# A dynamic convolution with LayerNorm and FFN: W1's last channels loaded as half rows in order, the first chunk summed by GpSimd and out of PSUM by VectorE, W1 split from PSUM, and a planner that lets transfers share engines

## The chip, the core and the metric

The kernel runs on one core of a Trainium2 chip. The metric is the device time of one execution in microseconds; the kernel before takes 903.2 us, the median of three runs (901.89 to 903.55).

## What is computed

```python
w = softmax(weight_gen, axis=-1)          # 8 x 4224 x 8 heads x 7 taps
x_pad = concat([zeros((B, 6, D)), x], 1)  # D = 192, 24 channels per head
y = einsum('bshk,bskhg->bshg', w, x_unf)  # each token: 7 taps over itself and the 6 tokens before
xn = (y - mean) / sqrt(var + 1e-6) * g_ln
out = y + relu(xn @ w_ch1) @ w_ch2        # 192 -> 768 -> 192
```

W1 and W2 come as 64-bit floats; the kernel reads them as pairs of 32-bit words and makes float32 of them. The products keep float32 accuracy with float16 operands: each operand is split into a high and a low half, and three products are summed.

## The kernel before

Each of the 128 partitions holds 264 consecutive tokens. They are worked in *parts* (six of 4 tokens, six of 8, fifteen of 12, then 8 and 4), each part in *chunks* of 4 or 6 tokens, and for the FFN in *groups* of 4 tokens, 66 in all.

A chunk (`conv`, L389) is seven products of x with the softmax weights in PSUM (tile wn), on VectorE: three pairs (taps 1 and 2, 3 and 4, 5 and 6) into tiles `pr`, of which there are five, and tap 0 into y. The sum: two accumulating DMAs issued by GpSimd (`pr<-pr`, L429) add one half of the first two pairs to the other, and four GpSimd additions (L426) bring everything into y. Then, per part, ScalarE takes sums and squares, and VectorE refines the reciprocal root in five small instructions (`newton`, L496 to L502); per group, ScalarE makes xh, its high half hl (L530), GpSimd the low half (L532), and a DMA transpose on SP's queue makes xT (three tiles). TensorE multiplies a group by W1 in three units of two PSUM banks (ph, two tiles); ScalarE and VectorE take each unit out (hh L576, hlo L578). W2's products go into po (L615 to L617), VectorE adds them to y (L628), and y goes out.

W1 (`load_weights`, L651; `weights`, L728) is three blocks of 128 rows in SBUF: channels 0 to 127, and twice a mix that pairs its rows with the last 64 channels, so that the wide products use all rows. The first load brings channels 0 to 127 (tile hh, 768 KB); the second (another hh, 384 KB) brings channels 128 to 191 as two sets of 64 rows, columns 0 to 383 on the upper partitions and 384 to 767 on the lower. `from_double` (L667) makes float32 of them, in PSUM first and then in tile hlo; ScalarE writes the high halves scaled by g and the scaled values themselves, GpSimd the low halves (L767), and twelve transfers on SP's queue (`shift`, L770) put the pieces into place. A first group can be transposed only behind them on that queue.

What sets the order: every operation is recorded with its engine, a cost and a due time, and `Plan.order` (L110) lays them out; engines, then, execute in the order that the plan gives. The due time is the token's number less a lead from the table WANT (two numbers per kind). The planner gives SP's and GpSimd's DMAs each a transfer line of its own, each 1.2 times as slow as alone, and keeps accumulating DMAs and transposes apart: neither starts while the other is under way, by waits in the program. SP's DMAs and ScalarE's use eight semaphores in turn, so each waits until the one eight before it has landed.

Of the kernel before, what the change touches and what calls it, by code (L numbers as in the profile page):

```python
# [16 lines left out]
P = 128  # L17
ALPHA = 8.0
NT = 4
# [3 lines left out]
EARLY = 0  # L23
CHUNK = 6
RING = 36
# [5 lines left out]
WANT = {'load': (-3.03, -19.38), 'wload': (75.89, -46.46), 'max': (34.08, -74.96), 'sub':  # L31
    (21.91, 116.2), 'exp': (-14.1, -87.13), 'sum': (39.61, 14.25), 'rcp': (47.36, -72.19),
    'inv': (5.5, -15.05), 'mul': (-41.29, 41.17), 'halo': (40.29, 5.8), 'c0': (31.82, 116.02),
    'c1': (-5.94, 64.81), 'c2': (-43.6, 83.75), 'c3': (-47.04, -21.22), 'd0': (9.3, 89.09),
    'd1': (-94.02, 26.89), 'a0': (-71.11, 94.32), 'a1': (-79.29, 54.26), 'a2': (-38.66, 25.11),
    'a3': (-85.55, -28.69), 'sums': (-195.22, -33.59), 'squares': (-140.38, 13.37), 'rstd':
    (10.58, 16.36), 'newton': (-103.15, -69.45), 'xh': (-25.48, -52.72), 'hi': (-57.47, -92.25),
    'lo': (-83.78, 4.64), 'turn': (28.46, -71.2), 'unit': (18.6, -32.95), 'relu': (-139.25,
# [3 lines left out]
    'w_load2': (-57.38, -12.17), 'w_as': (-60.92, -81.04), 'w_av': (-119.14, 5.54), 'w_an':  # L42
    (-33.01, 32.36), 'w_cs': (-238.15, 59.14), 'w_cv': (-62.73, -9.89), 'w_cn': (-11.28, 14.73),
    'w_c2s': (-60.02, 35.93), 'w_c2v': (-72.14, 39.45), 'w_c2n': (-110.82, -2.78), 'w_s1':
    (-187.12, 48.03), 'w_s2': (2.12, 17.57), 'w_h': (-21.92, -107.89), 'w_l': (-164.62, 27.59),
    'w_m': (-71.61, -95.38), 'w_h2': (13.94, -20.11), 'w_l2': (-164.98, -137.48)}
RAMP = 3.7
AHEAD = 0.0
WINDOW = 20.41
NEAR = 29.84  # L50
# [14 lines left out]
class Plan:  # L65
# [12 lines left out]
    def op(self, eng, cost, want, fn, r=(), w=(), lat=140.0, dma=0.0, kind=None):  # L78
# [5 lines left out]
        lead, more = WANT[want[0]]  # L84
        s = want[1]
        o.want = s - lead - more * max(0.0, 1 - s / RAMP)
# [21 lines left out]
    def order(self):  # L108
# [3 lines left out]
        last, clear = {"add": None, "turn": None}, {"add": 0.0, "turn": 0.0}  # L112
        for o in self.ops:
# [34 lines left out]
        while len(out) < len(self.ops):  # L148
# [22 lines left out]
            if o.dma:  # L171
# [3 lines left out]
                dma_free[o.eng] = begin + o.dma * (1.0 if o.kind == "turn" else 1.2)  # L175
# [16 lines left out]
def kernel(  # L192
# [61 lines left out]


# [9 lines left out]
    def dma_ns(n):  # L265
        return n * P / 250.0
# [7 lines left out]
    V.memset(bias[:, 0:1], 4e-6 / (ALPHA * ALPHA))  # L274
# [112 lines left out]

# [3 lines left out]
    def conv(c):  # L391
# [3 lines left out]
        prs = {k: Buf("pr") for k in (1, 3, 5)}  # L395
# [18 lines left out]
        def mul(k, nk):  # L414
# [4 lines left out]
            if k:  # L419
# [5 lines left out]
        def add(k, E=Q):  # L425
            E.tensor_tensor(out=flat(0), in0=flat(0), in1=flat(k), op=ALU.add)  # L426
# [4 lines left out]
        nd = n * D  # L431
# [3 lines left out]
        if c < EARLY:  # L435

            for i, (k, h) in enumerate(((1, 0), (1, 1), (3, 0), (3, 1), (5, 0), (5, 1))):
                op("Pool", q_ns(nd), (f"a{max(0, i - 2)}", t0), lambda k=k, h=h: add(k + h), [(prs[k], h)], yw)
            return
        for i, k in enumerate((1, 3)):  # L440
            op("Pool", 610, (f"d{i}", t0), lambda k=k: dma_add(k, k + 1), [(prs[k], 1)],
               [(prs[k], 0)], dma=600.0 + 400.0 * n, kind="add")
# [10 lines left out]
    def norm(pa):  # L453
# [29 lines left out]
        A2 = ALPHA / 2  # L483
# [6 lines left out]
        def root():  # L490
            A.activation(row(1), row(0), AF.Ln, scale=1.0 / (D * A2 * A2), bias=bias[:, 0:1])
            A.activation(row(1), row(1), AF.Exp, scale=-0.5)
            A.activation(row(2), row(1), AF.Square)

        def newton():
            V.tensor_scalar(out=aux(0), in0=row(0), scalar1=1.0 / (D * A2 * A2), scalar2=1e-6 / (A2 * A2),  # L496
                            op0=ALU.mult, op1=ALU.add)
            V.tensor_tensor(out=aux(1), in0=aux(0), in1=row(2), op=ALU.mult)
            for o in (aux(2), row(1)):
                V.scalar_tensor_tensor(out=o, in0=aux(1), scalar=3.0, in1=row(1), op0=ALU.subtract,  # L500
# [3 lines left out]
        op("ACT", 670, ("rstd", S0), root, vs, [(s4, "r")])  # L504
        op("V", 780, ("newton", S0), newton, [*vs, (s4, "r")], [(s4, "n"), "aux", *ms])
# [58 lines left out]
    W1S = ["h0", "l0", "h1b", "l1b", "l2t", "h2t"] + [(k, i) for k in ("h1t", "l1t", "h2b", "l2b") for i in range(2)]  # L564
# [75 lines left out]
    for name, shape, dt in (("g", [P, 2], F32), ("gi", [P, 2], F32), ("s1", [P, 4], F32),  # L640
                            ("s2", [P, 4], F32), ("r1", [P, 4], F32), ("r2", [P, 4], F32),
                            ("fs", [P, 1], F32), ("w1h", [P, 3, F], F16), ("w1l", [P, 3, F], F16),
                            ("w2h", [P, NF, D], F16), ("w2l", [P, NF, D], F16)):
        W[name] = cp.tile(shape, dt, name="c_" + name)
    for name in ("g", "s1"):
# [226 lines left out]
```

## Time and profile before

| | us |
|---|---|
| timed, three runs | 901.89, 903.2, 903.55 |
| profiled execution | 901.05 |
| its span | 899.2 |
| TensorE, VectorE, ScalarE, GpSimd busy | 813.2, 781.7, 675.7, 694.4 |
| first product of the first group | 53.02 |

The span runs from the first to the last instruction of the program. A busy TensorE isn't TensorE at its peak, since matmuls overlap: the count of matmuls in a stretch says more. An idle time stands with the instruction that follows it, and with what ended the wait.

### The profile page before, as it was taken

What the parts mean: (1) busy time and instruction counts of PE and PEld (TensorE: products, weight loads), DVE (VectorE), ACT (ScalarE), POOL (GpSimd) and SP (SyncE); (2) the same over time, 40 slices, a digit from 0 to 9 for tenths busy, and PEclk for the clock granted to TensorE, in tenths of its full rate; (3) what the DMA queues carried; (4) which work ended last, traced back from release to release, by engine and by line L of the source; (5) the groups of instructions that cost most, each with busy time, mean ns of one, the idle gap of its engine ahead of it and who ended that gap; (6) DMA issues with size and microseconds to landing.
All of it is one profiled execution on the core that took longest, in us unless ns stands there. A gap on an engine that the chain in (4) does not pass through costs nothing.

```text
span 899.2 us, 21468 instructions
## 1 busy us (share of the span) xinstructions
PE 813.2 (90%) x8716; PEld 728.8 (81%) x8716; DVE 781.7 (87%) x833; ACT 675.7 (75%) x1773; POOL 694.4 (77%) x403
## 2 busy tenths in 40 slices
PE   0037979999999999989999999999999999999997
PEld 0025969889898888888899988898899898889987
DVE  5799989999999999889999998999999799785332
ACT  1579877888878787788878778788788778788321
POOL 4499989998998896886987979689698598886000
PEclk9997999999999999999999999999999999999999
DMA  8875778878786878777788688787877867654212
GB/s 212 211 166 126 173 160 180 195 163 189 164 195 111 203 147 193 184 158 166 164 187 185 139 182 175 169 197 158 170 167 148 170 134 162 153 111 98 63 53 54
DMA packets 138604, 142.42 MB, mean 158 GB/s; under 512 B 107657, under 2 KB 109449, under 8 KB 138505
## 3 DMA queue, kind: packets, MB, share of 16 engines
q1 hardware_dynamic: 123513, 89.14, 42.0%
q0 software_dynamic: 14688, 51.91, 29.6%
q8 instruction: 68, 1.11, 0.5%
q14 instruction: 31, 0.25, 0.1%
q10 hardware_dynamic: 304, 0.00, 0.0%
HBM read 36.43 MB, written 25.95 MB: 69 GB/s over the span
## 4 chain that ended last, share of the span: by engine, by line
PE 26%; DVE 12%; POOL 9%; ACT 8%; DMA 6%; issue 5%; SPq 0%; POOLq 0%; DVEq 0%
PE ph L546 13%; POOL y L426 7%; DVE pr L423 7%; PE po L615 5%; PE po L617 4%; PE po L616 4%; DMA xT<-hl 3%; DVE hlo L578 3%; ACT hh L576 3%; ACT junk L468 2%; DMA pr<-pr 2%; ACT junk L463 1%; DVE y L423 1%; POOL hl L532 1%; DVE y L628 1%
## 5 line engine op out<-in xcount | busy, mean ns | idle before, releaser
L426 POOL TENSOR_TENSOR y<-y,pr 128x1152 f32<-128x1152 f32 (+1 forms) x204 | 503.6, 2475 | 82.0 <-DVE pr L423 70.5
L616 PE MATMUL po<-c_w2l,hh 128*128 128x192 f16 x1584 | 389.7, 246 | 1.4 <-POOL c_w2l L808 1.4
L615 PE MATMUL po<-c_w2h,hh 128*128 128x192 f16 x1584 | 390.1, 246 | 0.0
L617 PE MATMUL po<-c_w2h,hlo 128*128 128x192 f16 x1584 | 389.7, 246 | 0.0
L546 PE MATMUL ph<-xT,c_w1h 128*128 128x256 f16 x2376 | 328.3, 275 | 34.2 <-DMA xT<-hl 18.8
L423 DVE TENSOR_TENSOR pr<-x,wn 128x2304 f32<-128x2304 f32 (+1 forms) x153 | 337.4, 2215 | 8.3 <-DMA x<-in_x_dram 3.3
L546 PEld LDWEIGHTS <-c_w1h 128*128 128x128 f16 x2376 | 226.4, 98 | 76.4 <-issue 43.2
L578 DVE SCALAR_TENSOR_TENSOR hlo<-ph,hh 128x1024 f16<-128x1024 f32 x198 | 239.3, 1217 | 49.9 <-ACT hh L576 48.7
L576 ACT ACTIVATE hh<-ph 128x1024 f16<-128x1024 f32 x198 | 199.6, 1008 | 68.8 <-PE ph L546 46.0
L546 PE MATMUL ph<-xT,c_w1l 128*128 128x256 f16 (+1 forms) x1584 | 211.0, 274 | 9.8 <-DMA xT<-hl 8.9
L615 PEld LDWEIGHTS <-hh 128*128 128x128 f16 x1584 | 155.0, 98 | 7.8 <-issue 6.1
L616 PEld LDWEIGHTS <-hh 128*128 128x128 f16 x1584 | 155.1, 98 | 1.6
L617 PEld LDWEIGHTS <-hlo 128*128 128x128 f16 x1584 | 155.0, 98 | 1.6 <-issue 1.6
L514 ACT ACTIVATE xh<-y,s 128x192 f32<-128x192 f32 x264 | 123.3, 536 | 31.9 <-DVE s L502 28.3
L546 PEld LDWEIGHTS <-c_w1l 128*128 128x128 f16 (+1 forms) x1584 | 108.5, 96 | 41.8 <-issue 26.2
L532 POOL TENSOR_TENSOR hl<-xh,hl 128x768 f16<-128x768 f32 x66 | 118.8, 1868 | 15.9 <-ACT hl L530 15.8
L463 ACT ACTIVATE junk<-y 128x192 f32<-128x192 f32 x264 | 95.1, 360 | 42.4 <-POOL y L426 36.8
L468 ACT ACTIVATE junk<-y,s 128x192 f32<-128x192 f32 x264 | 119.5, 453 | 7.1
L429 POOL DMA_DIRECT2D pr<-pr x102 | 96.2, 1003 | 34.5 <-DVE pr L423 20.9
L628 DVE SCALAR_TENSOR_TENSOR y<-po,c_fs,y 128x384 f32<-128x384 f32 x132 | 79.8, 608 | 28.2 <-PE po L617 28.1
L530 ACT ACTIVATE hl<-xh 128x768 f16<-128x768 f32 x66 | 55.1, 835 | 8.2 <-DMA xT<-hl 7.6
L423 DVE TENSOR_TENSOR y<-x,wn 128x1152 f32<-128x1152 f32 (+1 forms) x51 | 60.0, 1178 | 0.0
(64 smaller groups left out, 327.2 us busy)
## 6 DMA issues: line engine op xcount, KB each, us to landing
pr<-pr POOLq DMA_DIRECT2D x60, 576.0 KB, 7.6
x<-in_x_dram SPq DMA_DIRECT2D x30, 576.0 KB, 7.0
out_dram<-y SPq DMA_DIRECT2D x30, 576.0 KB, 4.8
pr<-pr POOLq DMA_DIRECT2D x42, 384.0 KB, 6.6
out_dram<-y SPq DMA_DIRECT2D x21, 384.0 KB, 4.3
x<-in_x_dram SPq DMA_DIRECT2D x20, 384.0 KB, 6.6
w<-in_weight_gen_dram SPq DMA_DIRECT2D x21, 336.0 KB, 4.3
pr<-in_moe_w_ch_dram SPq DMA_DIRECT2D x1, 1152.0 KB
```

The costliest lines, as they stand in the source:

```text
L423: V.tensor_tensor(out=ov, in0=xv, in1=wv, op=ALU.mult)
L426: E.tensor_tensor(out=flat(0), in0=flat(0), in1=flat(k), op=ALU.add)
L463: A.activation(junk, at(y)[:, j, :], AF.Identity, scale=-1.0 / D, accum_out=at(s4)[:, 3, t : t + 1])
L468: A.activation(junk, at(y)[:, j, :], AF.Square, bias=at(s4)[:, 3, t : t + 1], accum_out=at(s4)[:, 0, t : t + 1])
L514: A.activation(at(xh)[:, t, :], at(y)[:, i, :], AF.Identity, bias=at(s4)[:, 3, g + t : g + t + 1], scale=at(s4)[:, 1, g + t : g + t + 1])
L532: lambda xh=xh, hl=hl: Q.tensor_tensor(out=halves(hl, True), in0=pairs(xh), in1=halves(hl, False), op=ALU.subtract),
L546: T_.matmul(at(gp["ph"][u])[:, r, v * 2 * P : (v + 1) * 2 * P], W[w][rows, wb, (2 * u + v) * P : (2 * u + v + 1) * P], xv[rows, r, xb, :, ...
L576: lambda: A.activation(at(hh)[:, us, :], at(ph), AF.Relu), [ph], [(hh, u)])
L578: lambda: V.scalar_tensor_tensor(out=at(hlo)[:, us, :], in0=at(ph), scalar=0.0, in1=at(hh)[:, us, :], op0=ALU.max, op1=ALU.subtract),
L615: T_.matmul(o, tok(hh, j), w2h[:, j, :], start=(j == 0), stop=False)
L616: T_.matmul(o, tok(hh, j), w2l[:, j, :], start=False, stop=False)
L617: T_.matmul(o, tok(hlo, j), w2h[:, j, :], start=False, stop=(j == NF - 1))
```

## The change

The second W1 load takes the half rows in the order of the tensor, so that a row's two halves lie on two neighbouring partitions; g's matching column is loaded in one transfer with each value twice. The float32 values of W1 stay in PSUM (ph for channels 0 to 127, po for the rest). The high halves are written from there as before; the low halves are now one VectorE instruction each (scale and subtract), the scaled copies are gone, and W1's high and low halves lie side by side in one tile, so that six transfers shift both at once, the last four picking every second partition.

Chunk 0 (`EARLY = 1`) has no accumulating DMAs: VectorE writes taps 5 and 6 into PSUM one by one and adds each to y, and GpSimd adds the other two pairs up among themselves and then to y. Newton's scaling is put into constants, which leaves four instructions, and the square goes to PSUM. The planner lets SP's and GpSimd's transfers that are under way together lengthen each other, knows of the eight semaphores, and the table WANT gives a lead at five token numbers; all its numbers are new.

```diff
-EARLY = 0
+EARLY = 1
...
-WANT = {'load': (-3.03, -19.38), 'wload': (75.89, -46.46), 'max': (34.08, -74.96), 'sub':
+KNOTS = (0, 4, 8, 16, 40)
+WANT = {'load': (169.34, 28.1, -223.88, -75.09, -80.57), 'wload': (125.01, 154.38, 150.29,
...
+            if o.dma:
+                before = lanes[o.eng == "Pool"]
+                if len(before) >= LANES:
+                    t = max(t, before[-LANES].end)
...
-                dma_free[o.eng] = begin + o.dma * (1.0 if o.kind == "turn" else 1.2)
+                dma_free[o.eng] = begin + o.dma
+                for e, x in latest.items():
+                    if e != o.eng and o.kind != "turn":
+                        both = min(max(0.0, dma_free[e] - begin), o.dma)
+                        dma_free[o.eng] += both
+                        dma_free[e] += both
...
+        if c < EARLY:
+            for i, k in enumerate((1, 3, 0)):
+                op("V", v_ns(2 * nd if k else nd), (f"c{i}", t0), lambda k=k: mul(k, 2 if k else 1),
+                   [*xr, "wn"], [(prs[k], 0), (prs[k], 1)] if k else yw)
+            for k in (5, 6):
+                ph = Buf("ph")
+                op("V", v_ns(nd), ("c3", t0), lambda k=k, ph=ph: mul(k, 1, ph), [*xr, "wn"], [ph])
+                op("V", v_ns(nd), ("c3", t0), lambda ph=ph: V.tensor_tensor(out=flat(0), in0=bank(ph)[:, :nd], in1=flat(0), op=ALU.add),
+                   [ph], yw)
+            for i, (a, b) in enumerate((((1, 0), (1, 1)), ((3, 0), (3, 1)), ((1, 0), (3, 0)), (None, (1, 0)))):
+                op("Pool", q_ns(nd), (f"a{i}", t0),
...
         def newton():
-            V.tensor_scalar(out=aux(0), in0=row(0), scalar1=1.0 / (D * A2 * A2), scalar2=1e-6 / (A2 * A2),
-                            op0=ALU.mult, op1=ALU.add)
-            V.tensor_tensor(out=aux(1), in0=aux(0), in1=row(2), op=ALU.mult)
+            V.scalar_tensor_tensor(out=aux(1), in0=row(0), scalar=D * 1e-6, in1=aux(0), op0=ALU.add, op1=ALU.mult)
...
         dma("SP", SY, "load", lambda: words(1, 0, F),
-            bass.AP(tensor=w1b.tensor, offset=P * 2 * F, ap=[[F, 2], [2 * F, 64], [1, F]]), 4 * F, raw[1])
+            bass.AP(tensor=w1b.tensor, offset=P * 2 * F, ap=[[F, P], [1, F]]), 4 * F, raw[1])
...
-        def low(dst, src, hi, n, r, w):
-            op("Pool", q_ns(n), ("w_l", 0), lambda: Q.tensor_tensor(out=dst(), in0=src(), in1=hi(), op=ALU.subtract), r, w)
+        def low(dst, src, scale, hi, n, r, w):
+            op("V", v_ns(n), ("w_l", 0), lambda: V.scalar_tensor_tensor(
+                out=dst(), in0=src(), scalar=scale, in1=hi(), op0=ALU.mult, op1=ALU.subtract), r, w)
...
-        halves(w1h, hc, [(raw[1], "h")], "h")
-        copy("w_h", lambda: f32(wa, F), lambda: f32(wa, F), F, ["gi"], [wa], gi[:, 0:1])
...
+        shift(w1[bot, 1], lambda: w1[top, 0], ["h0", "l0"], ["1b"])
+        shift(w1[top, 2], lambda: w1[bot, 0], ["h0", "l0"], ["2t"])
...
+            for dst, name in ((w1[top, 1, :, fs], "1t"), (w1[bot, 2, :, fs], "2b")):
+                shift(dst, lambda i=i: hlc()[i::2], [(raw[1], "h"), (raw[1], "l")], [(name, i)], F)
```

How the order moves, at three places. A number behind a name is the buffer; rows without a time stand in the order of their engine.

SP's queue at the start of the program, before (w: weights of the softmax, hh_88 and hh_89: W1's two loads):

```order
L341 DMA w_64<-in_weight_gen_dram 128x1x224
L323 DMA x<-in_x_dram 120x1x1920
L328 DMA x<-in_x_dram 8x768
L341 DMA w_65<-in_weight_gen_dram 128x1x448
L341 DMA w_66<-in_weight_gen_dram 128x1x672
L657 DMA hh_88<-in_moe_w_ch_dram 128x1536
L657 DMA hh_89<-in_moe_w_ch_dram 128x1x768
L341 DMA w_64<-in_weight_gen_dram 128x1x672
```

and in the changed kernel:

```order
L385 DMA w_64<-in_weight_gen_dram 128x1x224
L367 DMA x<-in_x_dram 120x1x1920
L372 DMA x<-in_x_dram 8x768
L710 DMA hh_88<-in_moe_w_ch_dram 128x1536
L710 DMA hh_89<-in_moe_w_ch_dram 128x768
L385 DMA w_65<-in_weight_gen_dram 128x1x448
L385 DMA w_66<-in_weight_gen_dram 128x1x672
L385 DMA w_64<-in_weight_gen_dram 128x1x672
```

W1's two loads stand ahead of the second and third w instead of behind them.

VectorE from chunk 0's first product on, before (L423: products; L361, L368: softmax; L689 to L699: W1 from double to float):

```order
L423 TENSOR_TENSOR pr_76<-x,wn_102 128x2x768
L423 TENSOR_TENSOR pr_77<-x,wn_102 128x2x768
L361 TENSOR_REDUCE mx_93<-w_65 128x64
L423 TENSOR_TENSOR y_67<-x,wn_102 128x768
L423 TENSOR_TENSOR pr_79<-x,wn_102 128x2x768
L368 TENSOR_REDUCE wn_102<-e_97 128x64
L689 TENSOR_SCALAR ph_103<-hh_88 128x768
L361 TENSOR_REDUCE mx_92<-w_66 128x96
L692 SCALAR_TENSOR_TENSOR ph_103<-hh_88,ph_103 128x768
L689 TENSOR_SCALAR ph_104<-hh_89 128x384
L695 SCALAR_TENSOR_TENSOR ph_103<-hh_88,ph_103 128x768
L692 SCALAR_TENSOR_TENSOR ph_104<-hh_89,ph_104 128x384
```

and in the changed kernel (L469: products, L485: sums out of PSUM, L744 to L754: W1):

```order
L469 TENSOR_TENSOR y_67<-x,wn_102 128x768
L469 TENSOR_TENSOR ph_103<-x,wn_102 128x768
L469 TENSOR_TENSOR ph_104<-x,wn_102 128x768
L485 TENSOR_TENSOR y_67<-ph_103,y_67 128x768
L485 TENSOR_TENSOR y_67<-ph_104,y_67 128x768
L744 TENSOR_SCALAR ph_103<-hh_88 128x768
L469 TENSOR_TENSOR pr_77<-x,wn_102 128x2x768
L747 SCALAR_TENSOR_TENSOR ph_103<-hh_88,ph_103 128x768
L750 SCALAR_TENSOR_TENSOR ph_103<-hh_88,ph_103 128x768
L754 SCALAR_TENSOR_TENSOR ph_103<-pr_78,ph_103 128x768
L405 TENSOR_REDUCE mx_93<-w_65 128x64
L744 TENSOR_SCALAR po_105<-hh_89 128x384
```

Chunk 0 begins with y and the two taps in PSUM, its product pairs (pr_77, and pr_79 in the next row) come later, behind pieces of W1's first load, and the second W1 load (hh_89) follows.

GpSimd around the low half of group 32, the third `hl` row, before (L426: sums into y, L429: accumulating DMAs, L363: softmax, L532: low halves):

```order
L532 TENSOR_TENSOR hl_83<-xh_81,hl_83 128x2x384
L532 TENSOR_TENSOR hl_84<-xh_82,hl_84 128x2x384
L426 TENSOR_TENSOR y_69<-y_69,pr_80 128x1152
L363 TENSOR_TENSOR e_96<-w_66,mx_92 128x672
L426 TENSOR_TENSOR y_69<-y_69,pr_80 128x1152
L532 TENSOR_TENSOR hl_83<-xh_81,hl_83 128x2x384
L426 TENSOR_TENSOR y_69<-y_69,pr_76 128x1152
L426 TENSOR_TENSOR y_69<-y_69,pr_78 128x1152
L429 DMA pr_77<-pr_77 128x1152
L429 DMA pr_79<-pr_79 128x1152
```

and in the changed kernel (L472, L475, L407, L584):

```order
L584 TENSOR_TENSOR hl_83<-xh_81,hl_83 128x2x384
L584 TENSOR_TENSOR hl_84<-xh_82,hl_84 128x2x384
L472 TENSOR_TENSOR y_72<-y_72,pr_78 128x1152
L407 TENSOR_TENSOR e_96<-w_66,mx_92 128x672
L584 TENSOR_TENSOR hl_83<-xh_81,hl_83 128x2x384
L475 DMA pr_77<-pr_77 128x1152
L472 TENSOR_TENSOR y_72<-y_72,pr_78 128x1152
L472 TENSOR_TENSOR y_72<-y_72,pr_76 128x1152
L475 DMA pr_80<-pr_80 128x1152
L475 DMA pr_79<-pr_79 128x1152
```

The transpose of group 32 waits for its low half and for the accumulating DMAs that the plan puts ahead of it. Before, there is none behind the low half that it waits for; now it is planned behind the three that follow (pr_77, pr_80, pr_79). The same comes again at groups 38, 44, 50 and 56.

More of the change, by code (lines that the diff above doesn't have):

```diff
@@ L18 @@
 ALPHA = 8.0
+ROOT_OF = (0.5 / (192 * ALPHA * ALPHA)) ** (1.0 / 3.0)
 NT = 4
@@ L53, with ahead_of @@
+AHEAD = 0.0
+WINDOW = 18.11
+NEAR = 19.46
+LANES = 8
+def ahead_of(key, s):
+    v = WANT[key]
+    for i in range(len(v) - 1):
+        if s < KNOTS[i + 1]:
+            return v[i] + (v[i + 1] - v[i]) * ((s - KNOTS[i]) / (KNOTS[i + 1] - KNOTS[i]))
+    return v[-1]
 class Buf:
@@ L174, in order @@
                             dma_free.get(o.eng, 0.0))
-                dma_free[o.eng] = begin + o.dma * (1.0 if o.kind == "turn" else 1.2)
+                dma_free[o.eng] = begin + o.dma
[4 more added lines that the diff above has]
+                        dma_free[e] += both
+                        x.end += both
+                        for d in x.nxt:
+                            d.ready = max(d.ready, x.end)
+                        if x.kind in clear:
+                            k = "turn" if x.kind == "add" else "add"
+                            clear[k] = max(clear[k], x.end)
+                latest[o.eng] = o
+                lanes[o.eng == "Pool"].append(o)
                 o.end = dma_free[o.eng] + self.DMA_END
@@ L562, in narrow_products @@
                        stop=(first and v == 1))
-    W1S = ["h0", "l0", "h1b", "l1b", "l2t", "h2t"] + [(k, i) for k in ("h1t", "l1t", "h2b", "l2b") for i in range(2)]
+    W1S = ["h0", "l0", "1b", "2t"] + [(k, i) for k in ("1t", "2b") for i in range(2)]
     def at_unit(unit):
@@ L786, in weights @@
-        shift(w1l[top, 2, :], lambda: w1l[bot, 0, :], ["l0"], ["l2t"])
-        copy("w_h", lambda: f32(wc, F2), lambda: f32(wc, F2), F2, ["gi"], [wc], gi[:, 1:2])
-        low(lc, lambda: f32(wc, F2), hc, F2, [wc, (raw[1], "h")], [(raw[1], "l")])
-        halves(w1l, lc, [(raw[1], "l")], "l")
+        def low(dst, src, scale, hi, n, r, w):
+            op("V", v_ns(n), ("w_l", 0), lambda: V.scalar_tensor_tensor(
+                out=dst(), in0=src(), scalar=scale, in1=hi(), op0=ALU.mult, op1=ALU.subtract), r, w)
@@ L791, in weights @@
+        shift(w1[top, 2], lambda: w1[bot, 0], ["h0", "l0"], ["2t"])
+        low(lambda: hlc()[:, 1], lambda: f32(wc, F2), gi[:, 1:2], lambda: hlc()[:, 0], F2, [wc, "gi", (raw[1], "h")],
+            [(raw[1], "l")])
+        for i in range(2):
+            fs = slice(i * F2, (i + 1) * F2)
+            for dst, name in ((w1[top, 1, :, fs], "1t"), (w1[bot, 2, :, fs], "2b")):
+                shift(dst, lambda i=i: hlc()[i::2], [(raw[1], "h"), (raw[1], "l")], [(name, i)], F)
         tn = NF // 3 * D
```

133 lines of the change are left out of this document (63 added, 70 removed), and 14 rows, old and new, of the table WANT.

## The prediction

> **What bounds the kernel now.** I read the page's first part, then the busy time by stretch, then the timeline of the start. The header of the stretches names each engine, its busy time and in brackets its instructions.
>
> ```profile
> span 899.2 us, 21468 instructions
> PE 813.2 (90%) x8716; PEld 728.8 (81%) x8716; DVE 781.7 (87%) x833; ACT 675.7 (75%) x1773; POOL 694.4 (77%) x403
> ...
> core 0: us, PE busy (x) PEld busy (x) DVE busy (x) ACT busy (x) POOL busy (x), PEclk, DMA share, GB/s
> ...
> 20.00:40.00 20.00, 0.59 (x2) 0.50 (x2) 12.81 (x23) 7.69 (x27) 8.21 (x7) 1.00 0.76 208
> 40.00:60.00 20.00, 6.52 (x45) 4.67 (x46) 19.35 (x32) 15.94 (x43) 17.50 (x12) 1.00 0.83 191
> 60.00:80.00 20.00, 9.51 (x56) 6.43 (x55) 19.69 (x28) 17.58 (x51) 19.24 (x13) 0.67 0.65 132
> 80.00:100.00 20.00, 18.62 (x202) 16.30 (x200) 18.73 (x27) 17.26 (x44) 20.00 (x14) 0.99 0.66 147
> 120.00:160.00 40.00, 35.29 (x380) 31.61 (x379) 37.06 (x45) 29.80 (x83) 35.92 (x25) 1.00 0.80 167
> 200.00:300.00 100.00, 98.58 (x1069) 88.80 (x1067) 97.38 (x102) 83.97 (x223) 89.96 (x53) 1.00 0.78 172
> 820.00:840.00 20.00, 20.00 (x220) 17.85 (x218) 8.68 (x14) 13.97 (x34) 4.74 (x3) 1.00 0.36 91
> ```
>
> With nothing to wait for (820 to 840 us) TensorE does 220 matmuls in 20 us, 11 per us. All 8716 at that rate are 792 us, so 107 us of the span are TensorE time lost, most of it before 80 us: 103 matmuls are done by then. From 80 us on TensorE is near its rate, but so is VectorE: busy 19.35, 19.69 and 18.73 of 20 us between 40 and 100, and 97.38 of 100 between 200 and 300. Up to 300 us the groups of tokens reach TensorE as fast as VectorE makes them. The start is where idle time is left:
>
> ```profile
> GB/s 0 77 133 288 199 225 263 313 272 243 250 229 236 268 180 37 53 50 108 298 384 305 253 250 253 255 254 224 209 240 98 155 72 67 261 172 283 250 225 205
> ...
> 26.75 0.56 DVE L689 TENSOR_SCALAR ph<-hh 128x384 int32<-128x384 int32 x1 [7.12 <-DMA hh<-in_moe_w_ch_dram]
> ...
> 49.67 1.55 SPq L536 DMA_TRANSPOSE xT<-hl  x1
> 53.02 1.44 PE L546 MATMUL ph<-xT,c_w1h 128*128 128x256 f16 x6 [18.76 <-DMA xT<-hl]
> ...
> 70.01 0.61 PE L546 MATMUL ph<-xT,c_w1l 64*128 64x256 f16 x4 [6.03 <-DMA xT<-hl]
> ...
> 81.57 0.24 PE L616 MATMUL po<-c_w2l,hh 128*128 128x192 f16 x1 [1.38 <-POOL c_w2l L808]
> ...
> 128.17 0.39 PE L546 MATMUL ph<-xT,c_w1l 64*128 64x256 f16 x4 [1.56 <-DMA xT<-hl]
> ```
>
> VectorE stands still for 7.12 us until W1's last 64 channels (tile hh, 384 KB) are there at 26.7 us. The first row is bytes per second in slices of 1.5 us from 0 to 60: around 13 to 21 us some 230 to 270 GB/s, then 37, 53 and 50 between 22.5 and 27. So the last load is not behind a full queue; it trickles by itself through a few transfer engines. TensorE begins at 53.02 with the first transposed group, and waits for groups again at 70.01 and 128.17.
>
> **The change, part by part.** Its durations, from the groups by shape, and the first and last of the twelve transfers that shift W1:
>
> ```profile
> L423 DVE TENSOR_TENSOR pr<-x,wn 128x1536 f32<-128x1536 f32 x63 | 108.9, 1745 | 6.7 <-DMA x<-in_x_dram 3.3 <-ACT rr L372 2.5 <-issue 0.5
> L423 DVE TENSOR_TENSOR y<-x,wn 128x768 f32<-128x768 f32 x21 | 19.7, 942 | 0.0
> L628 DVE SCALAR_TENSOR_TENSOR y<-po,c_fs,y 128x384 f32<-128x384 f32 x132 | 79.8, 608 | 28.2 <-PE po L617 28.1
> L699 DVE SCALAR_TENSOR_TENSOR hlo<-pr,ph 128x768 f32<-128x768 f32 x1 | 0.9, 946 | 0.0
> L699 DVE SCALAR_TENSOR_TENSOR hlo<-pr,ph 128x384 f32<-128x384 f32 x1 | 0.5, 544 | 0.0
> L496 DVE TENSOR_SCALAR wn<-s 128x12 f32<-128x12 f32 x15 | 2.4, 161 | 0.2
> L767 POOL TENSOR_TENSOR c_w1l<-hlo,c_w1h 128x768 f16<-128x768 f32 x1 | 1.6, 1630 | 0.0
> L767 POOL TENSOR_TENSOR hh<-hlo,hh 128x384 f16<-128x384 f32 x1 | 0.9, 905 | 0.0
> L429 POOL DMA_DIRECT2D pr<-pr x102 | 96.2, 1003 | 34.5 <-DVE pr L423 20.9 <-DMA xT<-hl 6.1 <-ACT c_r L716 3.1
> ...
> 41.41 1.17 SPq L770 DMA_DIRECT2D c_w1h<-c_w1h  x2
> 48.97 0.59 SPq L770 DMA_DIRECT2D c_w1l<-hh  x1
> ...
> 41.80 1.43 ACT L764 ACTIVATE hlo<-hlo,c_gi 128x768 f32<-128x768 f32 x2
> ```
>
> *The load.* W1's last channels are read as 128 half rows in their order instead of two sets of 64, and both W1 loads are issued ahead of the second and third w. The slices up to 12 us hold 2.25 MB, and the first w, x and W1 are 2.2 MB by their shapes; with 2 us to land I expect W1 on chip by about 14 us, when VectorE still has chunk 0 to do; the 7.12 us go. If the reordered load still lands late, nothing of this term is won; that end is kept. The Trainium skill, "DMA: Bandwidth & Descriptors", section "Why a DMA increments its semaphore by 16 and not by 1", says that a copy is split over the largest number of engines, up to 16, that divides the slowest dimension of both patterns. By it the old pattern (slowest dimension 2) runs on 2 engines and the new one on 16. The 37 to 53 GB/s agree with the first half; no run here shows the second.
>
> *Chunk 0 on VectorE.* One product pair (1.745) becomes two single products (2 x 0.942) into PSUM, and two sums out of PSUM come on top. A sum of that shape out of PSUM isn't in the trace: 0.942 as the same size in SBUF, 1.22 as twice the 608 ns of L628, half the size with one PSUM input. I take 0.942, the row of the right size: +1.88 - 1.75 + 1.88 = +2.0, at most +2.6. What GpSimd loses is two accumulating DMA issues (2 x 1.003).
>
> *W1's low halves* go from GpSimd (1.630 + 0.905) to VectorE: like L699, 0.946 + 0.544 = +1.5; the 608 ns of L628 against the 544 of L699, both 384 elements, price the PSUM source at below 0.1 more each. Two ScalarE copies (1.43 in sum, the last row above) go too; ScalarE is busy 15.94 of 20 us there, so I count them at nothing, and they would be worth at most their 1.43.
>
> *The shifts* become 6 transfers. The twelve hold SP's queue from 41.41 to 49.56, and the first transpose, queued behind them, is issued at 49.67. Six at about 0.6 us are 3.6: if the low halves are ready at about the same 42 us, the transpose waits for its own data, not for SP, and TensorE starts at some 50 instead of 53. That isn't added: the groups after it set the end.
>
> *Newton* loses one of five instructions, 0.16 us, in each of 29 parts. Twelve or thirteen parts lie before 300 us: -2.0. Behind that VectorE has idle time (8 us of the 92 after 354 us) and the saving is hidden.
>
> *Sum on VectorE up to 300 us:* -7.1 + 2.0 + 1.5 - 2.0 = **-5.6**. Bounds: -7.1 - 2.0 below if the PSUM work were free, +1.5 above if the load still comes late.
>
> *GpSimd.* It loses 2.0 + 2.5 us of work, but its first sums now wait for the product pairs, and VectorE does the single products and the sums out of PSUM ahead of those: five instructions of 0.942, 4.7 us. VectorE's products need the five pr buffers that GpSimd frees, so it will wait there once or twice after 65 us. That wait doesn't exist in the trace of before; between nothing and one sum (2.28 us, below) each, I take +1.0.
>
> *The steady part.* The order changes everywhere. What could be won is what TensorE loses there:
>
> ```profile
> 300.00:354.00 54.00, 51.47 (x555) 45.93 (x554) 50.98 (x51) 42.06 (x115) 43.19 (x23) 1.00 0.81 172
> 354.00:446.00 92.00, 88.76 (x962) 79.92 (x961) 83.78 (x79) 74.92 (x194) 77.69 (x42) 1.00 0.75 168
> ...
> 331.65 1.65 POOL L532 TENSOR_TENSOR hl<-xh,hl 128x768 f16<-128x768 f32 x1
> ...
> 341.06 1.34 POOL L429 DMA_DIRECT2D pr<-pr  x1
> ...
> 350.17 2.03 SPq L536 DMA_TRANSPOSE xT<-hl  x1
> ...
> 445.63 1.86 POOL L532 TENSOR_TENSOR hl<-xh,hl 128x768 f16<-128x768 f32 x1
> ...
> 468.87 0.82 PE L546 MATMUL ph<-xT,c_w1h 128*128 128x256 f16 x6
> ```
>
> At 11 per us these 555 and 962 matmuls are 50.5 and 87.5 us, so 3.5 and 4.5 are lost, 8.0 in all. One cause is seen for group 23: its low half ends at 333.3, but three accumulating DMAs are planned ahead of its transpose, the third is issued at 341.06, and the transpose leaves at 350.17. In the new order groups 23 and 26 are free of this, 25 and 20 wait for an add one row behind, and groups 32, 38, 44, 50 and 56 get the long form. I take -1.5 of the 8.0.
>
> **Forecast:** -5.6 + 1.0 - 1.5 = -6.1 us. The profiled execution took 901.05 us with its 1.85 us around the span; that gives 895.0. The median of the timed runs, 903.2, stands 2.15 above it, and I forecast that median: **897.1 us**. Chance 0.50, its own range 893 to 900.5.
>
> **Rivals.** *GpSimd becomes the bound.* For: it is busy 19.24 and 20.00 of 20 us between 60 and 100 us. Against: only 35.92 of 40 between 120 and 160, and 89.96 of 100 later, so it can catch up. Its own sum is -4.5 us of work and about half of the 4.7 us of later start, which it can't fill with other work, +2.5 as an estimate, -2.0 in all: 899.0, as a median 901.2. Chance 0.18. How its sums stretch:
>
> ```profile
> L426 POOL TENSOR_TENSOR y<-y,pr 128x768 f32<-128x768 f32 x4 | 7.2, 1805 | 2.2 <-DMA pr<-pr 1.2 <-DVE pr L423 1.0
> L426 POOL TENSOR_TENSOR y<-y,pr 128x768 f32<-128x768 f32 x14 | 31.7, 2282 | 0.7 <-DMA pr<-pr 0.5
> ```
>
> The first row is 16 to 27 us, where VectorE stood idle for 7, the second 60 to 100 us, where it was full. With VectorE filled, the four sums of chunk 0 could take 2.28 each, 1.9 us more. The Trainium skill, "GPSIMD Engine Reference", section "1. Specifications", has GpSimd's SBUF interface shared with VectorE and contended for by VectorE instructions with two SBUF inputs. By that rule the 1.9 us come, the sums out of PSUM excepted; it speaks for this rival, and the two rows agree with it, though DMA issues between the sums may stretch them too.
>
> *The steady losses go as well:* all 8.0 instead of 1.5 give -12.6, 888.4, as a median 890.6. For: the groups that lost most are re-ordered. Against: new long waits come in. Chance 0.13.
>
> *Slower: the five transposes behind adds decide.* Before, group 32's low half ended at 447.5 and TensorE began with it at 468.87, 21.4 us later. With group 23's detour (16.9 us from its low half to its transpose, and 3.4 until TensorE has it, as after 49.67) it would be there after 20.3. The margin is 1.1 us: the third add came 7.8 us behind the low half there, and from about 9 us on each further us is TensorE's. At 3 us late in each of five groups that is +15 - 6.1 = +8.9: 910.0, as a median 912. For: GpSimd's DMA issues wait for VectorE's products in the trace (20.9 us in all at L429). Against: group 23 itself was just in time. Chance 0.14.
>
> *The load is not faster:* W1's last channels again land at about 25 us, because of the traffic of the other loads. VectorE then only gains Newton's 2.0 and pays 3.5: +1.5, and with the rest 902 to 904. Against it are the 37 to 53 GB/s. Chance 0.05.
>
> **Chances.** Faster by over 0.2% (under 901.4; 0.2% is about what a measurement of this kernel can tell from no change): the forecast, the steady gain, and six tenths of the GpSimd case, 0.74. Within it: the rest of that case and the load's, 0.12. Slower: 0.14. The range reaches from the steady gain, 889, to 904; most of the slower case is left out.
>
> **What would show it.** VectorE's wait for hh (7.1 us) gone and W1's last load landed before 16 us; sums out of PSUM (128x768) of 0.94 to 1.22 us; TensorE's first group at about 50 us; VectorE over 95% busy from 15 to 300 us, with a few us waiting for GpSimd's pr. Wrong would be: a new wait of VectorE for GpSimd above 4 us before 100 us; TensorE waits for transposed groups around 470, 540, 615, 690 and 765 us; or a PSUM product that takes much longer than in SBUF.

## The result, and the profile after

The changed kernel takes **910.8 us** (median of four runs, 909.87 to 911.86), the kernel before 902.7 in the same session (901.89 to 903.55): a ratio of 1.009, with a 95% interval of 1.0072 to 1.0107. The forecast was 897.1 with a range up to 904. It is slower by 0.9%, and the forecast had the wrong sign.

The profile of the changed kernel begins:

```profile
span 908.9 us, 21412 instructions
...
PE 819.0 (90%) x8716; PEld 731.3 (80%) x8716; DVE 785.8 (86%) x809; ACT 671.9 (74%) x1771; POOL 692.0 (76%) x399
```

The start comes as early as forecast. In the changed kernel's timelines, ScalarE's and then VectorE's and TensorE's, W1's last channels are there at 12.5 us:

```profile
12.52 1.33 ACT L741 ACTIVATE pr<-hh 128x384 f32<-128x384 f32 x2 [6.80 <-DMA hh<-in_moe_w_ch_dram]
```

```profile
10.32 1.82 DVE L469 TENSOR_TENSOR ph<-x,wn 128x768 f32<-128x768 f32 x2
12.04 1.94 DVE L485 TENSOR_TENSOR y<-ph,y 128x768 f32<-128x768 f32 x2
13.91 0.95 DVE L744 TENSOR_SCALAR ph<-hh 128x768 int32<-128x768 int32 x1
...
19.88 0.55 DVE L744 TENSOR_SCALAR po<-hh 128x384 int32<-128x384 int32 x1
```

```profile
48.49 6.58 PE L598 MATMUL ph<-xT,c_w 128*128 128x256 f16 x40 [17.09 <-DMA xT<-hl]
...
62.97 1.36 PE L598 MATMUL ph<-xT,c_w 64*128 64x256 f16 x7 [5.07 <-DMA xT<-hl]
```

VectorE's L744 rows have no bracket: it waits for neither load. TensorE starts at 48.49 instead of 53.02. Busy time by stretch, in the changed kernel:

```profile
20.00:40.00 20.00, 0.59 (x2) 0.61 (x3) 19.04 (x30) 9.61 (x34) 17.17 (x12) 1.00 0.72 175
...
60.00:80.00 20.00, 12.42 (x83) 8.87 (x84) 18.80 (x17) 11.88 (x35) 16.66 (x11) 0.66 0.64 138
...
200.00:300.00 100.00, 93.98 (x997) 83.60 (x995) 93.34 (x96) 79.08 (x211) 87.19 (x51) 0.98 0.80 168
...
354.00:446.00 92.00, 91.58 (x987) 82.38 (x985) 85.80 (x84) 75.93 (x196) 78.26 (x42) 1.00 0.72 165
```

VectorE is busy 19.04 of 20 us between 20 and 40 (before 12.81). But where all engines were full before, between 200 and 300 us, VectorE, GpSimd and TensorE have all become idler: TensorE does 997 matmuls instead of 1069, and VectorE, at 93.34 of 100 us, is below the 95% that the prediction gave as a sign. Coarser stretches, first of the kernel before and then of the changed one, show where time is won and lost:

```profile
0.00:160.00 160.00, 90.52 (x897) 77.86 (x898) 138.67 (x191) 109.65 (x300) 128.16 (x92) 0.96 0.78 176
160.00:300.00 140.00, 137.12 (x1488) 123.41 (x1486) 136.52 (x144) 118.18 (x320) 129.01 (x79) 1.00 0.78 172
300.00:450.00 150.00, 144.22 (x1552) 129.09 (x1550) 137.90 (x133) 120.50 (x317) 124.88 (x66) 1.00 0.78 171
450.00:700.00 250.00, 248.96 (x2702) 224.74 (x2701) 236.89 (x228) 201.92 (x531) 209.16 (x111) 1.00 0.80 169
```

```profile
0.00:160.00 160.00, 95.79 (x936) 81.46 (x937) 146.11 (x190) 109.83 (x304) 125.21 (x88) 0.96 0.69 159
160.00:300.00 140.00, 132.26 (x1405) 117.58 (x1403) 131.50 (x135) 111.31 (x301) 124.41 (x77) 0.99 0.81 170
300.00:450.00 150.00, 147.37 (x1589) 132.45 (x1588) 139.60 (x130) 124.29 (x330) 127.44 (x68) 1.00 0.78 170
450.00:700.00 250.00, 241.21 (x2599) 217.02 (x2597) 226.37 (x211) 191.79 (x507) 200.84 (x106) 1.00 0.77 170
```

Against before, TensorE has done 39 matmuls more by 160 us, then 83 fewer, 37 more, and 103 fewer. At 11 per us the last is 9.4 us, and all four together are 10.0. So the loss lies in the steady part, where the prediction looked for a gain. The waits there (what waited, for whom: us in total, times, longest), first of before:

```profile
PE ph L546 <- DVE hlo L578: 16.2, 17, 3.1
...
ACT rr L372 <- DVE pr L423: 3.4, 2, 2.7
ACT rr L372 <- DVE y L423: 2.1, 3, 1.5
```

and of the changed kernel:

```profile
PE ph L598 <- DVE hlo L630: 26.9, 29, 4.6
...
ACT wn L547 <- DVE pr L469: 19.0, 15, 2.2
ACT rr L416 <- DVE pr L469: 18.4, 11, 3.7
```

TensorE waits longer for VectorE's low halves `hlo`, which free its PSUM tile ph. From 450 to 700 us alone, first before and then changed:

```profile
PE ph L546 <- DVE hlo L578: 0.2, 1, 0.2
```

```profile
PE ph L598 <- DVE hlo L630: 8.8, 11, 2.2
```

The 8.6 us more are most of the 9.4 us lost there. And ScalarE waits for VectorE's products `pr` at two places: at the square into wn (L547), a wait that before does not have, and at the softmax's Ln (L416, out rr), 18.4 us instead of 3.4. One wait of the latter kind, from VectorE's, ScalarE's and TensorE's timelines:

```profile
641.48 0.86 DVE L412 TENSOR_REDUCE wn<-e 128x96 f32<-128x672 f32 x1 [0.53 <-ACT e L410]
642.43 2.56 DVE L469 TENSOR_TENSOR pr<-x,wn 128x2304 f32<-128x2304 f32 x1
646.62 1.23 DVE L630 SCALAR_TENSOR_TENSOR hlo<-ph,hh 128x1024 f16<-128x1024 f32 x1 [1.63 <-ACT hh L628]
```

```profile
645.02 0.34 ACT L416 ACTIVATE rr<-wn,bias 128x96 f32<-128x96 f32 x1 [3.58 <-DVE pr L469]
645.39 0.28 ACT L417 ACTIVATE rr<-rr 128x96 f32<-128x96 f32 x1
645.58 1.00 ACT L628 ACTIVATE hh<-ph 128x1024 f16<-128x1024 f32 x1
```

```profile
647.90 1.36 PE L598 MATMUL ph<-xT,c_w 128*128 128x256 f16 x11 [1.63 <-DVE hlo L630]
```

The sums (L412) are done at 642.34. The Ln needs nothing else, but starts at 645.02, when the *next* product has ended (642.43 + 2.56 = 644.99). Behind it in ScalarE's queue stands the relu hh, then VectorE's hlo, then TensorE, which stands still for 1.63 us. A square does the same, in ScalarE's timeline:

```profile
577.82 0.18 ACT L547 ACTIVATE wn<-s 128x12 f32<-128x12 f32 x1 [2.21 <-DVE pr L469]
577.94 1.92 ACT L628 ACTIVATE hh<-ph 128x1024 f16<-128x1024 f32 x2
```

There TensorE then loses 2.18 us. Why a product that only reads weights holds these up can be read from the code: weights, sums and Newton's rows are columns of one PSUM tile, wn, and in the program any access of one engine to it waits for the accesses of the other that are written ahead of it, reads behind reads too. In the changed kernel 12 of the 23 Ln stand behind a product in this way, before it is 8, and 22 of the 29 squares, before none (the square went to SBUF). The plan's own dependences don't have this wait: it orders as if the Ln depended on the sums alone.

### The profile page after: what moved, and what is told of

It is laid out like the page before. It is cut to its first block, busy times and chain, and to the rows that moved or that the text cites. A ratio compares the mean times of both kernels' runs of the same rounds, so it can differ in the third digit from the quotient of the medians.

```text
span 908.9 us, 21412 instructions
## 1 busy us (share of the span) xinstructions
PE 819.0 (90%) x8716; PEld 731.3 (80%) x8716; DVE 785.8 (86%) x809; ACT 671.9 (74%) x1771; POOL 692.0 (76%) x399
## 5 line engine op out<-in xcount | busy, mean ns | idle before, releaser
L472 POOL TENSOR_TENSOR y<-y,pr 128x1152 f32<-128x1152 f32 (+1 forms) x201 | 490.5, 2442 | 74.1 <-DVE pr L469 60.2
L598 PE MATMUL ph<-xT,c_w 128*128 128x256 f16 (+1 forms) x3960 | 439.8, 275 | 53.9 <-DVE hlo L630 26.9
L598 PEld LDWEIGHTS <-c_w 128*128 128x128 f16 (+1 forms) x3960 | 334.9, 98 | 134.3 <-issue 77.9
L469 DVE TENSOR_TENSOR pr<-x,wn 128x2304 f32<-128x2304 f32 (+1 forms) x152 | 336.3, 2220 | 6.8 <-ACT wn L547 2.6
L628 ACT ACTIVATE hh<-ph 128x1024 f16<-128x1024 f32 x198 | 198.8, 1008 | 71.4 <-PE ph L598 48.5
L584 POOL TENSOR_TENSOR hl<-xh,hl 128x768 f16<-128x768 f32 x66 | 114.6, 1741 | 19.4 <-ACT hl L582 19.3
L475 POOL DMA_DIRECT2D pr<-pr x100 | 91.6, 993 | 39.1 <-DVE pr L469 18.5
L469 DVE TENSOR_TENSOR y<-x,wn 128x1152 f32<-128x1152 f32 (+1 forms) x51 | 60.3, 1182 | 4.3 <-DMA x<-in_x_dram 2.8
L518 ACT ACTIVATION_READ_ACCUMULATOR junk<-y 128x1 f32 x264 | 49.4, 187 | 0.0
L523 ACT ACTIVATION_READ_ACCUMULATOR junk<-y,s 128x1 f32 x264 | 49.4, 187 | 0.0
```

The lines of the kernel that those rows point to most:

```text
L469: V.tensor_tensor(out=ov, in0=xv, in1=wv, op=ALU.mult)
L472: Q.tensor_tensor(out=flat(to), in0=flat(to), in1=flat(k), op=ALU.add)
L518: A.activation(junk, at(y)[:, j, :], AF.Identity, scale=-1.0 / D, accum_out=at(s4)[:, 3, t : t + 1])
L523: A.activation(junk, at(y)[:, j, :], AF.Square, bias=at(s4)[:, 3, t : t + 1], accum_out=at(s4)[:, 0, t : t + 1])
L584: lambda xh=xh, hl=hl: Q.tensor_tensor(out=halves(hl, True), in0=pairs(xh), in1=halves(hl, False), op=ALU.subtract),
L598: T_.matmul(at(gp["ph"][u])[:, r, v * 2 * P : (v + 1) * 2 * P], W[w][rows, wb, (2 * u + v) * P : (2 * u + v + 1) * P], xv[rows, r, xb, :, ...
```

## The experiments

The kernel before ran beside each batch, with medians of 901.6 to 903.8 us; times below are medians, each with its ratio to before.

**The load alone.** e3 is the kernel before with only the new load (half rows in order, g to match, shifts that pick every second partition); e4 is the changed kernel with the old load.

```diff
-    bass.AP(tensor=w1b.tensor, offset=P * 2 * F, ap=[[F, 2], [2 * F, 64], [1, F]])
+    bass.AP(tensor=w1b.tensor, offset=P * 2 * F, ap=[[F, P], [1, F]])
...
```

> The kernel before with only the load of W1's last 64 channels changed to half rows in their order (g's column and the source rows of the four last shifts follow), same order on every engine. If the prediction's term of the load is right, VectorE's wait of 7.1 us at 26.7 us goes, the load lands before 18 us, and the time falls by 5 to 7 us, to 896 to 898. If the start is not what sets the end (the gain is used up by waits further on), the wait goes but the time stays within 2 us of 902.7.

> The changed kernel with the old pattern of that load (two sets of 64 half rows), same order on every engine. If the load's pattern is what makes it slow, it lands at some 20 to 25 us instead of 12.5, VectorE waits there again, and the start is late by 5 to 10 us: 914 to 919 us if the start sets the end, 911 if waits further on take it up.

Measured: e3 895.8 us (0.9921, interval 0.9895 to 0.9947), e4 917.2 (1.0156, 1.0128 to 1.0183). The load is worth 7.9 us put in and 6.4 taken out. In e3 VectorE waits no more for the last channels, and TensorE starts at 45.63 us instead of 53.02. In e4 they come at 21.28 instead of 12.5 us (ScalarE's timeline), and TensorE starts at 52.63 instead of 48.49:

```profile
21.28 1.32 ACT L741 ACTIVATE pr<-hh 128x384 f32<-128x384 f32 x2 [15.51 <-DMA hh<-in_moe_w_ch_dram]
```

So the rest of the change costs some 15 us (895.8 to 910.8).

**The square, first try.** e1 puts the changed kernel's square back in SBUF, e2 puts the square of before into PSUM and VectorE's first Newton result into SBUF.

```diff
-A.activation(aux(0), row(1), AF.Square)          # e1, changed kernel
+A.activation(row(2), row(1), AF.Square)
-V.tensor_scalar(out=aux(0), in0=row(0), ...)     # e2, kernel before
+V.tensor_scalar(out=row(2), in0=row(0), ...)
```

> The changed kernel with one thing undone: ScalarE's square in rstd goes to the SBUF tile s4 again instead of into the PSUM tile wn, with the same order on every engine. Theory A (the square into wn makes ScalarE wait for VectorE's products that read wn, 21 us in the trace of after, and what is queued behind it, the relu of a unit, comes late): those waits go, TensorE's waits for hlo after 82 us fall from 45 towards the 33 us of before, and the time falls to 899 to 904 us. Theory B (the new order of the steady part is what costs, whatever ScalarE waits for): the time stays at 909 to 911 us.

> The kernel before with one thing added: ScalarE's square goes into the PSUM tile wn (and VectorE's scaled sum into s4 in its place), same order on every engine, five Newton instructions as before. Theory A: ScalarE waits for VectorE's products at most of the 29 squares, 15 to 20 us in all, and the time rises to 907 to 912 us. Theory B: 902 to 904 us.

Measured: e1 927.1 (1.0265, 1.0233 to 1.0296), e2 935.4 (1.0355, 1.0317 to 1.0393). Both theories missed in both runs, since both edits brought something else. Groups by shape, VectorE's first Newton instruction in e1, in e2 and in the changed kernel:

```profile
L550 DVE SCALAR_TENSOR_TENSOR wn<-s 128x12 f32<-128x12 f32 x15 | 23.3, 1553 | 0.7
```

```profile
L496 DVE TENSOR_SCALAR s<-s 128x12 f32<-128x12 f32 x15 | 22.9, 1525 | 0.0
```

```profile
L550 DVE SCALAR_TENSOR_TENSOR wn<-s,wn 128x12 f32<-128x12 f32 x15 | 2.6, 171 | 1.7 <-ACT wn L547 1.2 <-ACT rr L416 0.3
```

Twelve elements take 1.55 us with both inputs in SBUF (e1), 1.53 from SBUF to SBUF (e2), and 0.17 with one input in PSUM. These two runs say nothing of the square.

**Newton as a whole.** e5 is the changed kernel with the Newton part of before (five instructions, square in SBUF, first result in PSUM). e6 is e3 with the changed Newton part. Neither changes the order of the rest.

```diff
-A.activation(aux(0), row(1), AF.Square)
-V.scalar_tensor_tensor(out=aux(1), in0=row(0), scalar=D * 1e-6, in1=aux(0), ...)
+A.activation(row(2), row(1), AF.Square)
+V.tensor_scalar(out=aux(0), in0=row(0), ...)
+V.tensor_tensor(out=aux(1), in0=aux(0), in1=row(2), op=ALU.mult)
```

> The changed kernel with the Newton part of before: five instructions, the square back in SBUF, VectorE's first instruction from SBUF to PSUM; the order of all engines stays. Theory A (ScalarE's square into the PSUM tile waits for VectorE's queue, 15 waits of together 19.0 us, and holds up the relus behind it): the wait of ScalarE's square on VectorE is gone and the time falls from 910.8 to 899 to 905 us. Theory B (the new order of the steady part costs the time): 909 to 914 us, since nothing of the order changes and VectorE has one more small instruction of 0.16 us in each of 29 parts.

> The kernel before with the half rows (895.8 us by itself) and the Newton part of the change: four instructions, the square into PSUM; the order of all engines stays that of before. Theory A: waits of the square on VectorE appear and the time rises to 903 to 911 us. Theory B: 893 to 896 us, one instruction of 0.16 us less in each of 29 parts and no harm.

Measured: e5 908.0 (1.0058, 1.0035 to 1.0081), e6 900.2 (0.9972, 0.9959 to 0.9986). The shorter Newton *costs* 2.8 us in the changed kernel and 4.4 in e3. It has one instruction less in each part; what it adds is the square's wait. But that is not the whole loss: e5 and e6 both lie between the two theories' ranges. No run takes away the square's wait and nothing else, so that the wait is what costs is read from the traces, not shown by a run.

**Code against order.** e7 has the changed code with the planner, its costs and its table of before; e8 has e3's code with the new planner and table.

```diff
-        o.want = want[1] - ahead_of(*want)                                       # e7; e8 the other way
+        lead, more = WANT[want[0]]
+        s = want[1]
+        o.want = s - lead - more * max(0.0, 1 - s / RAMP)
...
```

> The code of the change (half rows, chunk 0 split, W1 from PSUM, Newton with the square in PSUM), but the planner's rules, costs of transfers and table of before. Theory A: the waits of the square stay, 902 to 912 us. Theory B: 888 to 896 us, below the 895.8 of before with the half rows alone, since Newton is shorter and the order is the old one.

> The code of before with the half rows (895.8 us by itself), but the planner's rules, costs of transfers and table of the change. Theory A (the square): no wait of the square on VectorE, 893 to 899 us. Theory B (the order): 905 to 913 us, with TensorE's steps between groups 30 and 60 longer, as in the changed kernel.

Measured: e7 900.9 (0.998, 0.9969 to 0.9992), e8 924.7 (1.0251, 1.0233 to 1.0269). With the code held, the new order costs 9.9 us (900.9 to 910.8). e7 lies between the two theories' ranges: the order costs, and the square as well. e8 goes far beyond what either theory gave; its table was made for other code.

**The Ln's wait.** e9 (the changed kernel), e10 (e5) and e12 (e8) let ScalarE's Ln read a copy of the sums in SBUF, so that it doesn't touch wn. e11 is e7 with the Newton part of before, e13 is e11 with the copies.

```diff
 V.tensor_reduce(out=sm, in_=at(e)[:, :m], axis=AX.X, op=ALU.add)
+V.tensor_copy(out=sb[:, :m], in_=sm)
-A.activation(at(rr)[:, :m], sm, AF.Ln, bias=bias[:, 1:2])
+A.activation(at(rr)[:, :m], sb[:, :m], AF.Ln, bias=bias[:, 1:2])
```

> The changed kernel, where VectorE copies the softmax's sums from the PSUM tile wn to SBUF (one copy of 96 elements after each sum, 23 in all, by an estimate from VectorE's other instructions of that size 0.2 us each) and ScalarE's Ln reads the copy. The order of all engines stays. Theory C: in the new order a product of VectorE that reads wn stands between a sum and ScalarE's Ln (12 of 23 Ln wait for one, 18.4 us in all; before 8, 3.4 us), and what ScalarE has queued behind it (relu) is late for TensorE. By it these waits go and the time falls from 910.8 to 903 to 908 us; the square's waits on products stay. Theory D (the order costs the time in other ways, and ScalarE's waits are only where it idles anyway): 910 to 915 us, up to 4.6 us more for the copies.

> The same with the Newton part of before too (square and Newton as in the run that gave 908.0 us), so that ScalarE touches wn nowhere in the steady part. Theory C: both kinds of waits gone, 896 to 903 us. Theory D: 907 to 912 us.

> The code of the change with the planner and the table of before (900.9 us) and with the Newton part of before: what is left of the change is the half rows, chunk 0's sums and W1 out of PSUM. If Newton costs here what it cost in the kernel before with the half rows (4.4 us, 895.8 to 900.2), this gives 895 to 898 us and chunk 0 and W1 cost next to nothing. If chunk 0 and W1 cost something that was hidden: 898 to 902 us.

> The code of before with the half rows and the new planner and table (924.7 us; there ScalarE's Ln waited 30.3 us for VectorE's products), with the sums copied to SBUF for the Ln. Theory C: 908 to 917 us. Theory D: 922 to 928 us.

> The code that gave 899.3 us (the change with the sums copied to SBUF and the Newton part of before, so that ScalarE waits for no product), but with the planner and the table of before. It tells what the new order costs or brings beside those waits: if nothing, 897 to 901 us (897.5 without the copies, which are 5.8 us of VectorE and partly hidden); if the new order is better where its waits are gone, 902 to 905 us; if it is worse in other ways too, 893 to 896 us.

Measured: e9 903.5 (1.0013, 0.9993 to 1.0032), e10 899.3 (0.9957, 0.9938 to 0.9977), e11 897.5 (0.9951, 0.9933 to 0.9968), e12 918.2 (1.0184, 1.0156 to 1.0212), e13 898.6 (0.9962, 0.9944 to 0.998). Although 23 copies were added (21 of 0.257 us, 5.8 us of VectorE in all), the changed kernel wins 7.3 us, and with the old Newton too 11.4. The waits of e10, and its stretch from 450 to 700 us:

```profile
PE ph L609 <- DVE hlo L641: 17.4, 20, 4.6
...
ACT rr L424 <- DVE sums L418: 8.9, 11, 1.5
```

```profile
450.00:700.00 250.00, 247.97 (x2687) 223.72 (x2685) 234.75 (x233) 203.37 (x532) 208.77 (x110) 1.00 0.80 171
```

TensorE's wait for hlo is down from 26.9 to 17.4 us, and 88 of the 103 lost matmuls are back. e10 and e13 differ in the order alone, with ScalarE's waits for products gone in both, and take the same time (899.3 and 898.6, the intervals of the ratios nearly the same, some 2 us to either side). So on balance the new order has cost nothing that these runs can tell beside these waits. The balance has two parts: by 160 us e10 has done 45 matmuls more than e13 (940, 895), and between 160 and 300 us 31 fewer (1431, 1462). In e12 theory C has the sign right, at 6.4 us, but the time lies 1.2 us above its range: e8 also loses at its start (1263 matmuls by 200 us, e3 1376), and why is open.

**The tile.** e14 is e5, e15 is e3, both with wn as two PSUM tiles of one bank: the weights of a softmax's first tokens in one, its last tokens, the sums and Newton's rows in the other.

```diff
-pool("wn", 1, [P, 2 * HALF], F32, pp)
+pool("wn", 2, [P, HALF], F32, pp)
...
+             lambda: [V.tensor_tensor(out=t_[:, : (b - a) * K].rearrange("p (m k) -> p m k", k=K),
+                                      in0=at(e)[:, a:b], in1=wide(sm)[:, a:b], op=ALU.mult)
+                      for t_, a, b in ((WNA, 0, cut(pa) * H), (WNB, cut(pa) * H, m)) if b > a],
...
```

> The changed kernel with the Newton part of before (908.0 us), and the PSUM tile wn as two tiles of one bank each: the weights of the first tokens of a softmax in one, those of its last tokens with the sums and Newton's rows in the other; the weights are written by two instructions instead of one in 21 of the 23 softmaxes (some 0.1 us more each, an estimate from 0.854 us for 672 elements, 0.623 for 448 and 0.395 for 224). The order stays. If ScalarE's Ln waits for a product because both use the same tile, as the program has it (in 11 of the 12 cases the product reads columns of the other bank only), the time falls to 896 to 901 us, as with the copies (899.3). If the wait has another cause, 906 to 910 us.

> The kernel before with the half rows (895.8 us) and the same two tiles. There only 3.4 us of ScalarE's waits for products can go, and 2 us of VectorE come: 893 to 898 us by every theory; it is run as a candidate for the fastest.

Measured: e14 897.8 (0.9942, 0.9924 to 0.996), **e15 892.7 (0.9884, 0.9866 to 0.9902)**, the fastest of all and below both kernels (0.3 us below its range too). A wait of e5, and then the waits of e14:

```profile
ACT rr L416 <- DVE pr L469: 18.7, 11, 3.6
```

```profile
PE ph L608 <- DVE hlo L640: 17.0, 17, 4.6
...
ACT rr L420 <- DVE wn L416: 6.3, 6, 1.5
ACT rr L420 <- DVE pr L476: 2.4, 1, 2.4
```

The Ln still reads PSUM, and the product that came between still runs ahead of it; the tile differs (and the weights are written in two pieces), and of 18.7 us of waits for products (e5) 2.4 are left. The waits came from the shared tile. In 11 of the 12 cases of the changed kernel the product reads the first bank alone, the Ln the second. The Trainium skill, "PSUM — Partial Sum Buffer", section "Terms", says that two engines must not be on one bank at once, reads against reads included. By that rule the wait was needed in one of the 12 cases; e14 agrees as far as the others go, and no run here shows two engines on one bank.

The two runs stand side by side, and e14 takes 5.1 us more than e15. So with the waits gone and the Newton part of before, what is left of the change beside its load (chunk 0, W1 out of PSUM, the order) still costs time. The largest loss lies between 160 and 300 us: e14 does 1400 matmuls there, the changed kernel 1405, e15 1487. Most of the 83 that the changed kernel lost there are thus not due to ScalarE's waits, and what they are due to stays open.

## Why the prediction was wrong

Two of its terms failed, Newton and the steady part. The load came out; what chunk 0, W1's low halves and the shifts are worth by themselves isn't shown.

- **Load: right.** -7.1 forecast, -7.9 (e3) and -6.4 (e4) measured, landed at 12.5 us where about 14 was said. With the old pattern in e4, the mean busy share of the core's 16 transfer engines is 0.13 from 18 to 20 us, at 48 GB/s: as much as two full engines. That agrees with the 2 engines that the prediction took from the Trainium skill ("DMA: Bandwidth & Descriptors", section "Why a DMA increments its semaphore by 16 and not by 1"); the 16 for the new pattern aren't shown.
- **Chunk 0 and W1's low halves: priced well, the total not shown.** A sum out of PSUM takes 0.954 us where 0.942 was taken, the low halves 1.009 and 0.608, 1.6 together where 1.5 was said. The prices were better than their reason: the rows that stood for work in SBUF have an input in PSUM themselves (wn in L423, ph in L699), so the comparison of L628 with L699 priced nothing of PSUM. All of it, with GpSimd's term, was +4.5; e11 less e3 is +1.7, but as a balance: by 300 us e11 has done 57 matmuls fewer than e3, and 68 more between 300 and 450 us, so neither term is shown apart. GpSimd's +1.0 did not come: in the first 100 us VectorE has no wait for it.
- **Shifts: the time came out, their part in it isn't shown.** TensorE starts at 48.49 where 50 was said. But e3, with the twelve shifts of before, starts at 45.63, and e4, with the six, at 52.63: what moves the start is the load.
- **Newton: failed.** -2.0 forecast, +2.8 to +4.4 measured (e5, e6). The step counted the instruction that goes; to the move of the square to PSUM, a part of the change, it gave no price. VectorE's instruction does go; ScalarE's square in its place stands behind whole products, 15 waits of 19.0 us, and the relu behind it is late.
- **Steady part: failed, and decided the sign.** -1.5 forecast, +9.9 measured for the order (e7 to the changed kernel). The step looked at one kind of order, transposes against accumulating DMAs, and took a gain there. It did not look at what stands between a sum and its Ln on VectorE. Without the waits there, the order is worth nothing on balance (e10, e13).

Together: -7.9 for the load, +1.7 for chunk 0 and W1, +3.4 for Newton (e11 to e7), +9.9 for the order, +7.1 in all; +8.1 was measured. These runs were timed in batches; by their ratios to the kernel before, which ran in each, the steps are -7.1, +2.7, +2.6 and +9.9, and add up to the +8.1. The +2.7 isn't clear of noise, the other three are.

The rival that was slower gave 912, close to 910.8, by a mechanism that did not happen. It put TensorE's waits at transposed groups from 470 us on; between 450 and 800 us the changed kernel's waits have these two of TensorE (PEld: its weight load) for another engine or a transfer:

```profile
PE ph L598 <- DVE hlo L630: 10.0, 14, 2.2
...
PEld L598 <- DMA xT<-hl: 0.4, 1, 0.4
```

For the transposed xT that is 0.4 us, once.

So its number came near by chance. The signs of a wrong forecast that the prediction listed (VectorE waiting for GpSimd, TensorE for transposes, a slow product into PSUM) don't hold either; the engine that waited was ScalarE, 75% busy, for whose waits the prediction had no term.

## What to carry to other kernels

When a change moves a result into a tile that another engine uses, or moves work between a producer and its consumer in such a tile, look up every access to that tile on both engines: the program may make a small instruction wait for a long one that it shares no data with, and everything queued behind it waits as well. An engine with a quarter of its time idle can still be the one that sets the end, if it waits in front of the instruction that frees TensorE's PSUM. Give data with different readers tiles of their own: here that was worth 10 us in the changed kernel with the Newton part of before (e5 to e14) and 3 us in the one before (e3 to e15).

## What the hardware showed beside that

VectorE's first Newton instruction, with all its operands in SBUF, had very different times in place: in e1 a mean of 1.55 us for 12 elements, in e2 1.53, and 0.17 where one input or the output is in PSUM. Over all 29 of e1's, the trace gives least, median and most, in ns:

```profile
L550 DVE SCALAR_TENSOR_TENSOR wn<-s x29: 160/1234/4029, 39.5 to 859.5; 128x12 f32<-128x12 f32 x15, 128x4 f32<-128x4 f32 x7, 128x8 f32<-128x8 f32 x7
```

The least is the time with PSUM; the rest is a wait inside the instruction that the profile books as busy. It is a wait for GpSimd, as the longest one shows (e1's timelines of VectorE and GpSimd):

```profile
102.70 4.03 DVE L550 SCALAR_TENSOR_TENSOR wn<-s 128x4 f32<-128x4 f32 x1
```

```profile
104.27 2.41 POOL L472 TENSOR_TENSOR y<-y,pr 128x768 f32<-128x768 f32 x1
```

The one ends at 106.73, the other at 106.68. In the same way, 27 of the 29 in e1 and 22 of the 29 in e2 run beside a GpSimd addition or subtraction, and each of them ends 0.03 to 0.05 us after one has ended; the other nine meet none and take 0.16 to 0.18 us. The Trainium skill, "GPSIMD Engine Reference", section "1. Specifications", has VectorE's instructions with two SBUF inputs, or in a two-port mode, contend with GpSimd for the SBUF interface. The traces agree for e1's, which has two SBUF inputs; whether e2's, which has one, runs in such a mode isn't shown. Together the 29 take 40.4 us of VectorE in e1 and 35.3 in e2, against some 5 at 0.17 each. e1 is 16 us slower than the kernel it came from and e2 32, more than any term of the change itself; in e2 the moved square has its own part in that, 6.3 us of waits for VectorE's products.
